# A decode step with grouped-query attention and a gated FFN: shorter tail arithmetic, an earlier drain of the last scores, and a repacked on-chip memory

## The chip, the core and the metric

The kernel runs on one core of one Trainium2 chip. The metric is the device time of one execution in microseconds (us), as the median of several. The profile is one execution seen by the hardware profiler; its span is about 1.7 us shorter than the device time of the same execution (708.6 and 710.3 for the kernel before).

## The reference

One token (x has shape 1x1x512) passes a layernorm, attention over a cache of 65,536 positions with 32 query and 8 key/value heads of 128, an output projection, a residual, a second layernorm and a gated FFN of width 1792:

```python
h  = x + A_ref(layernorm(x), k_cache, v_cache, wq, wo)      # softmax(q k / sqrt(128)) v, then wo
h2 = h + B_ref(layernorm(h), w_gate, w_up, w_down)          # (sigmoid(h wg) * (h wu)) wd
```

The caches are bf16, 134 MB each; all reads together are 282 MB. Streaming them is nearly all of the work.

## The kernel before

K and V come in 128 chunks of 2 MB (8 groups, 8 chunks of each kind per group), each as 128 rows of 16 KB, one per partition. One queue, the sync engine's, issues all of them in a fixed order. PE transposes each K chunk, DVE and ACT copy the result out of PSUM, and PE then multiplies by q ("T" and "S" below, S three blocks behind T). V chunks are multiplied by the softmax weights. The parts that the change touches:

```python
# tensors are placed one behind the other, in this order
x_row_b = SB([1, D], BF16);  x_row = SB([1, D], FP32);  xsq_row = SB([1, D], FP32)
...
h_row = SB([1, D], FP32);  h2_row = SB([1, D], FP32)
...
out_row_b = SB([1, D], BF16)
wo_sb = SB([P, H, D], BF16, "wo_sb")
# then 3 K buffers (the FFN weights lie over them), 6 staging tiles, 4 V buffers

# PE: the last three S blocks of a group are issued only when its V begins
def v_chunk(nv):
    if g not in v_started:
        drain_S((g + 1) * SBG)
        ...
# sync engine: FFN weights may land when the last S is done; V loads stand behind them
if fl and i >= idx_ffn:
    sp.wait_ge(sem_sprog, NSB)
    sp.dma_start(dst, srcap).then_inc(sem_wffn, 16)

# down projection: one row of 512, hT stationary
for f in range(NFC):
    mm = pe.matmul(ps_misc[0:1, 0:D], hT_b[:, f:f + 1], wd_sb[:, f, :], ...)
v.tensor_tensor(out=out_row_b, in0=ps_misc[0:1, 0:D], in1=h_row, op=ALU.add)
```

## Time and profile before

| | before |
|---|---|
| median of four runs, us | 710.65 (710.09 to 711.82) |
| span of the profiled run, us | 708.6 |
| mean DMA rate over the span, GB/s | 401 |
| busy share PE / DVE / ACT | 78% / 44% / 22% |
| last V chunk landed, us into the span | 688.7 |

A busy PE at 78% does not set the time here: the DMA engines are busy in nearly every slice. The views themselves are in the prediction below.

### The profile page before, as it was taken

How to read it: one execution, taken by the hardware profiler on the slowest of the kernel's cores; microseconds unless marked ns; L12 is line 12 of the kernel's file. 1: busy time of each engine (PE TensorE's matmuls, PEld its weight loads, DVE VectorE, ACT ScalarE, POOL GpSimd, SP SyncE). 2: the span in 40 equal slices, each digit the busy share in tenths (PEclk: the TensorE clock that was granted, in tenths of full speed). 3: DMA queues.
4: the chain of work that ended last, by engine and by line, in shares of the span. 5: the costliest groups of instructions: out<-in, count | busy, mean ns of one | idle time of the engine just before them, and what ended most of it. 6: DMA issues, size and time to landing. Idle time of an engine off the chain costs nothing.

```text
span 708.6 us, 26822 instructions
## 1 busy us (share of the span) xinstructions
PE 551.1 (78%) x12622; PEld 530.0 (75%) x12622; DVE 312.8 (44%) x498; ACT 158.9 (22%) x199; POOL 0.7 (0%) x7
## 2 busy tenths in 40 slices
PE   2987998869997798969887799869888689874235
PEld 2977998868996688968887788869788689863232
DVE  1755744427442654417442564417444464331002
ACT  0232522204221321204121222104122141212000
POOL 0000000000000000000000000000000000000000
PEclk9999877869777898869886697867877697765556
DMA  8999999999999999999999999999999999979970
GB/s 368 411 396 413 424 423 426 421 424 417 424 424 422 392 425 423 425 425 402 425 425 423 390 422 426 425 422 394 424 425 423 404 417 425 425 316 415 412 313 1
DMA packets 26162, 284.05 MB, mean 401 GB/s; under 512 B 2242, under 2 KB 8132, under 8 KB 9156
## 3 DMA queue, kind: packets, MB, share of 16 engines
q1 hardware_dynamic: 25780, 280.24, 94.6%
q8 instruction: 99, 1.62, 0.9%
q10 hardware_dynamic: 272, 2.10, 0.8%
q14 instruction: 11, 0.09, 0.0%
HBM read 282.33 MB, written 0.00 MB: 398 GB/s over the span
## 4 chain that ended last, share of the span: by engine, by line
PE 46%; DMA 44%; issue 6%; DVE 4%; ACT 0%; SPq 0%; DVEq 0%
DMA kin<-in_A_k_cache_dram 34%; PE ps_tr L576 28%; DMA v<-in_A_v_cache_dram 9%; PE ps_s L601 8%; PE ps_o L673 7%; DVE kts L408 1%; DVE pmax L442 1%; PE ps_misc L479 1%; DVE s L432 1%; PE ps_misc L721 1%; PE ps_misc L506 0%; ACT pt L532 0%; PE ps_misc L710 0%; PE ps_misc L715 0%; DVE diag L454 0%
## 5 line engine op out<-in xcount | busy, mean ns | idle before, releaser
L576 PE MATMUL ps_tr<-ident_b,kin 128*128 128x128 bf16 x4096 | 379.1, 246 | 60.1 <-issue 30.0
L408 DVE COPY kts<-ps_tr 128x1024 bf16<-128x1024 bf16 x384 | 258.3, 691 | 299.7 <-PE ps_tr L576 299.5
L576 PEld LDWEIGHTS ps_tr<-ident_b,kin 128*128 128x128 bf16 x4096 | 284.6, 110 | 68.5 <-issue 39.3
L419 ACT ACTIVATE kts<-ps_tr 128x1024 bf16<-128x1024 bf16 x128 | 130.8, 1022 | 469.5 <-PE ps_tr L576 469.5
L601 PE MATMUL ps_s<-qt_b,kts 128*128 128x4 bf16 x4096 | 184.5, 167 | 3.9 <-issue 3.7
L601 PEld LDWEIGHTS ps_s<-qt_b,kts 128*128 128x128 bf16 x4096 | 173.4, 102 | 1.8 <-issue 1.5
L673 PE MATMUL ps_o<-pt,v 128*128 128x4 bf16 x4096 | 119.6, 168 | 59.5 <-DMA v<-in_A_v_cache_dram 46.5
L673 PEld LDWEIGHTS ps_o<-pt,v 128*128 128x128 bf16 x4096 | 114.1, 98 | 65.4 <-DMA v<-in_A_v_cache_dram 48.0
L432 DVE COPY s<-ps_s 128x512 f32<-128x512 f32 x32 | 21.8, 681 | 10.7 <-PE ps_s L601 10.7
L532 ACT ACTIVATE pt<-s,nmax 128x512 bf16<-128x512 f32 x32 | 22.6, 710 | 14.7 <-DVE nmax L465 14.7
L515 DVE RECIPROCAL rs<-ps_misc 128x4 f32<-128x4 f32 x8 | 1.4, 174 | 46.9 <-PE ps_misc L684 46.9
L442 DVE TENSOR_REDUCE pmax<-s 128x4 f32<-128x2048 f32 x8 | 18.3, 2284 | 0.0
L735 ACT ACTIVATE stats<-stats,eps_c 1x1 f32<-1x1 f32 x1 | 0.3, 293 | 50.5 <-DVE stats L389 50.5
L499 PE MATMUL ps_misc<-ident_f,pmax 128*4 128x128 f32 x8 | 2.4, 297 | 11.5 <-DVE pmax L442 11.5
L479 PE MATMUL ps_misc<-wo_sb,aot_b 128*1 128x512 bf16 x32 | 9.9, 438 | 0.9 <-DVE aot_b L518 0.5
L499 PEld LDWEIGHTS ps_misc<-ident_f,pmax 128*4 128x4 f32 x8 | 0.6, 81 | 12.2 <-DVE pmax L442 12.2
L491 DVE TENSOR_TENSOR h_row<-ps_misc,h_row 1x512 f32<-1x512 f32 x7 | 4.8, 679 | 9.6 <-PE ps_misc L479 9.6
L555 PE MATMUL ps_misc<-xnT_b,wq_sb 128*128 128x1 bf16 x128 | 3.5, 165 | 6.5 <-DMA wq_sb<-in_A_wq_dram 6.5
L555 PEld LDWEIGHTS ps_misc<-xnT_b,wq_sb 128*128 128x128 bf16 x128 | 3.5, 104 | 6.6 <-issue 6.6
L532 ACT ACTIVATION_READ_ACCUMULATOR pt<-s,nmax 128x1 f32 x32 | 6.0, 189 | 0.0
L548 PE MATMUL ps_misc<-ident_b,xn_row_b 1*128 1x1 bf16 x4 | 0.3, 166 | 6.8 <-DVE xn_row_b L397 6.8
L548 PEld LDWEIGHTS ps_misc<-ident_b,xn_row_b 1*128 1x128 bf16 x4 | 0.2, 103 | 6.8 <-DVE xn_row_b L397 6.8
(51 smaller groups left out, 51.3 us busy)
## 6 DMA issues: line engine op xcount, KB each, us to landing
kin<-in_A_k_cache_dram SPq DMA_DIRECT2D x64, 2048.0 KB, 19.7
v<-in_A_v_cache_dram SPq DMA_DIRECT2D x64, 2048.0 KB, 24.2
wo_sb<-in_A_wo_dram SPq DMA_DIRECT2D x4, 1024.0 KB, 14.5
wq_sb<-in_A_wq_dram ACTq DMA_DIRECT2D x1, 2048.0 KB, 9.9
wq_sb<-in_A_wq_dram SPq DMA_DIRECT2D x1, 2048.0 KB, 12.2
wg_sb<-in_B_w_gate_dram SPq DMA_DIRECT2D x2, 896.0 KB, 7.7
wu_sb<-in_B_w_up_dram SPq DMA_DIRECT2D x2, 896.0 KB, 20.8
wd_sb<-in_B_w_down_dram SPq DMA_DIRECT2D x2, 896.0 KB, 21.9
```

The source lines that it names most:

```text
L408: v.tensor_copy(kt_stage[ss][:, :, :], ps_tr[bank][:, :].rearrange("p (t m) -> p t m", m=P)).then_inc(sem_evD, 1)
L419: act.activation(kt_stage[ss][:, :, :], ps_tr[bank][:, :].rearrange("p (t m) -> p t m", m=P), ACTF.Copy).then_inc(sem_evA, 1)
L432: v.tensor_copy(s_sb[sidx][:, :, b * BT:(b + 1) * BT], src).then_inc(sem_sevac, 1)
L442: v.tensor_reduce(out=pmax[sidx][:, :], in_=s_sb[sidx][:, :, :], axis=AX.X, op=ALU.max).then_inc(sem_pmax, 1)
L479: mm = pe.matmul(ps_misc[0:1, 0:D], aot_b[:, h:h + 1], wo_sb[:, h, :], start=(hh == 0), stop=(hh == R - 1))
L491: v.tensor_tensor(out=h_row[:, :], in0=ps_misc[0:1, 0:D], in1=h_row[:, :], op=ALU.add).then_inc(sem_hacc, 1)
L532: act.activation(pt_sb[sidx][:, j, :], s_sb[sidx][:, j, :], ACTF.Exp, bias=nmax[sidx][:, j:j + 1], scale=1.0, accum_out=rowsum[sidx][:, j: ...
L555: mm = pe.matmul(ps_misc[:, C_QT + h:C_QT + h + 1], wq_sb[:, c, h * P:(h + 1) * P], xnT_b[:, c:c + 1], start=(c == 0), stop=(c == NDC - 1))
L576: mm = pe.transpose(ps_tr[bank][:, i * P:(i + 1) * P], kin_buf[slot][:, t, :], ident_b[:, :])
L601: mm = pe.matmul(ps_s[bank][:, col:col + R], src_tiles[i], qt_b[:, g * R:(g + 1) * R], start=True, stop=True)
L673: mm = pe.matmul(ps_o[:, 0:R], v_buf[slot][:, t, :], pt_sb[sidx][:, :, tg], start=(tg == 0), stop=(tg == TG - 1))
L721: mm = pe.matmul(ps_misc[0:1, 0:D], hT_b[:, f:f + 1], wd_sb[:, f, :], start=(f == 0), stop=(f == NFC - 1))
```

## The change

The intent is to shorten what follows the last byte (layernorm by batch-norm statistics, down projection with the weights stationary, so that 56 one-column matmuls take the place of 14 of 512 columns) and to let the FFN weights start sooner (the last scores are drained right behind the last K chunk). Rows that are no longer needed are dropped, small tensors are added, and a pad is placed ahead of `wo_sb`.

```diff
-        x_row = SB([1, D], FP32, "x_row")
-        xsq_row = SB([1, D], FP32, "xsq_row")
...
-        h2_row = SB([1, D], FP32, "h2_row")
...
-        out_row_b = SB([1, D], BF16, "out_row_b")
+        hresT = SB([P, NDC], FP32, "hresT")
+        oT_f = SB([P, NDC], FP32, "oT_f")
+        out4_b = SB([NDC, P], BF16, "out4_b")
+        SB([P, 48], BF16, "pad0")
         wo_sb = SB([P, H, D], BF16, "wo_sb")
...  layernorm_row: two 512-element passes and three 1-element operations become
+            v.bn_stats(stats[:, 0:6], src)
+            v.bn_aggr(stats[:, 6:8], stats[:, 0:6])
...  k_chunk
+                if kc == NKC - 1:
+                    drain_S(NSB)
...  before the second layernorm's transposes: the residual is transposed too
+            for c in range(NDC):
+                mm = pe.matmul(ps_misc[:, C_HT + c:C_HT + c + 1], h_row[0:1, c * P:(c + 1) * P], ones_f[0:1, 0:1], ...)
...
-            for f in range(NFC):
-                mm = pe.matmul(ps_misc[0:1, 0:D], hT_b[:, f:f + 1], wd_sb[:, f, :], ...)
+            for blk in range(NDC):
+                for f in range(NFC):
+                    mm = pe.matmul(ps_misc[:, C_DN + blk:C_DN + blk + 1], wd_sb[:, f, blk * P:(blk + 1) * P], hT_b[:, f:f + 1], ...)
...  then add (128x4), transpose (4x128), copy, store as four rows
```

More of the change, by code (lines that the diff above doesn't have):

```diff
@@ L25 @@
     K_MODE="pe",
+    KDMA_FIRST=0,
+    V_EARLY=0,
+    V_EARLY_AT=2,
     V_QUEUE="sp",
@@ L83, in bass_sequential_preLN__gqa_block_cached__glu_gated_glu__decode_kernel @@
         modes = [kmode] * NKC
+    for kc in range(min(NKC, plan["KDMA_FIRST"])):
+        modes[kc] = "dma"
     assert all(m in ("pe", "dma") for m in modes)
@@ L108, in bass_sequential_preLN__gqa_block_cached__glu_gated_glu__decode_kernel @@
         x_row_b = SB([1, D], BF16, "x_row_b")
-        x_row = SB([1, D], FP32, "x_row")
-        xsq_row = SB([1, D], FP32, "xsq_row")
-        stats1 = SB([1, 8], FP32, "stats1")
-        stats2 = SB([1, 8], FP32, "stats2")
+        stats1 = SB([1, 16], FP32, "stats1")
+        stats2 = SB([1, 16], FP32, "stats2")
         xn_row_b = SB([1, D], BF16, "xn_row_b")
@@ L174, in bass_sequential_preLN__gqa_block_cached__glu_gated_glu__decode_kernel @@
         C_U = C_G + NFC
-        assert C_U + NFC <= 512
+        C_HT = C_U + NFC
+        C_DN = C_HT + NDC
+        C_OT = C_PMAXT
+        assert C_DN + NDC <= 512
         sem_kin = [SEM(f"sem_kin{i}") for i in range(NKIN)]
@@ L194, in bass_sequential_preLN__gqa_block_cached__glu_gated_glu__decode_kernel @@
         sem_hnT = SEM("sem_hnT")
+        sem_hTpe = SEM("sem_hTpe")
+        sem_hTc = SEM("sem_hTc")
+        sem_oTsb = SEM("sem_oTsb")
+        sem_oT = SEM("sem_oT")
         sem_ffn1 = SEM("sem_ffn1")
@@ L351, in _ @@
             idx_ffn = order.index(("V", G - 1, 0))
+            n_vearly = min(plan["V_EARLY"], NV, NCH) if (G > 1 and plan["V_QUEUE"] == "sp") else 0
             for i, (kind, g, c) in enumerate(order):
@@ L355, in _ @@
                     nk += 1
+                    if nk == plan["V_EARLY_AT"]:
+                        for j in range(n_vearly):
+                            issue_v(sp, j)
                 else:
-                    if plan["V_QUEUE"] == "sp":
+                    if plan["V_QUEUE"] == "sp" and nv >= n_vearly:
                         issue_v(sp, nv)
@@ L374, in _, with layernorm_row @@
             sp.wait_ge(sem_outsb, 1)
-            sp.dma_start(out[0, :, :], out_row_b[:, :]).then_inc(sem_out, 16)
+            sp.dma_start(out[0, 0, :].rearrange("(b p) -> b p", p=P), out4_b[:, :]).then_inc(sem_out, 16)
             sp.wait_ge(sem_out, 16)
-        def layernorm_row(v, src, dst_row32, dst_b, stats, sem_chain, sem_sqrt):
-            v.tensor_scalar(out=dst_row32[:, :], in0=src, scalar1=1.0, scalar2=0.0, op0=ALU.mult, op1=ALU.add,
-                            accum_out=stats[:, 0:1]).then_inc(sem_chain, 1)
+        def layernorm_row(v, src, dst_b, stats, sem_chain, sem_sqrt):
+            v.bn_stats(stats[:, 0:6], src).then_inc(sem_chain, 1)
@@ L381, in layernorm_row @@
             v.wait_ge(sem_chain, 1)
-            v.tensor_tensor_reduce(out=xsq_row[:, :], in0=dst_row32[:, :], in1=dst_row32[:, :], scale=1.0, scalar=0.0,
-                                   op0=ALU.mult, op1=ALU.add, accum_out=stats[:, 1:2]).then_inc(sem_chain, 1)
-            v.wait_ge(sem_chain, 2)
-            v.tensor_scalar(out=stats[:, 2:3], in0=stats[:, 0:1], scalar1=1.0 / D, scalar2=None, op0=ALU.mult).then_inc(sem_chain, 1)
+            v.bn_aggr(stats[:, 6:8], stats[:, 0:6]).then_inc(sem_chain, 1)
@@ L386, in layernorm_row @@
+            v.wait_ge(sem_sqrt, 1)
+            v.reciprocal(stats[:, 9:10], stats[:, 8:9]).then_inc(sem_chain, 1)
             v.wait_ge(sem_chain, 3)
-            v.tensor_tensor(out=stats[:, 3:4], in0=stats[:, 2:3], in1=stats[:, 2:3], op=ALU.mult).then_inc(sem_chain, 1)
+            v.tensor_scalar(out=stats[:, 10:11], in0=stats[:, 6:7], scalar1=-1.0, scalar2=stats[:, 9:10],
+                            op0=ALU.mult, op1=ALU.mult).then_inc(sem_chain, 1)
             v.wait_ge(sem_chain, 4)
-            v.tensor_scalar(out=stats[:, 4:5], in0=stats[:, 1:2], scalar1=1.0 / D, scalar2=stats[:, 3:4],
-                            op0=ALU.mult, op1=ALU.subtract).then_inc(sem_chain, 1)
@@ L391, in layernorm_row @@
-            v.wait_ge(sem_sqrt, 1)
-            v.reciprocal(stats[:, 6:7], stats[:, 5:6]).then_inc(sem_chain, 1)
-            v.wait_ge(sem_chain, 6)
-            v.tensor_scalar(out=stats[:, 7:8], in0=stats[:, 2:3], scalar1=-1.0, scalar2=stats[:, 6:7],
-                            op0=ALU.mult, op1=ALU.mult).then_inc(sem_chain, 1)
-            v.wait_ge(sem_chain, 7)
-            return v.tensor_scalar(out=dst_b[:, :], in0=dst_row32[:, :], scalar1=stats[:, 6:7], scalar2=stats[:, 7:8],
+            return v.tensor_scalar(out=dst_b[:, :], in0=src, scalar1=stats[:, 9:10], scalar2=stats[:, 10:11],
@@ L486, in f @@
                 if g == 0:
-                    v.wait_ge(sem_ln1, 8)
-                    v.tensor_tensor(out=h_row[:, :], in0=ps_misc[0:1, 0:D], in1=x_row[:, :], op=ALU.add).then_inc(sem_hacc, 1)
+                    v.wait_ge(sem_x, 16)
+                    v.tensor_tensor(out=h_row[:, :], in0=ps_misc[0:1, 0:D], in1=x_row_b[:, :], op=ALU.add).then_inc(sem_hacc, 1)
                 else:
@@ L543, in _ @@
         def _(pe):
-            pe.wait_ge(sem_ln1, 8)
+            pe.wait_ge(sem_ln1, 5)
             pe.wait_ge(sem_dsetup, 1)
@@ L700, in _ @@
             dve_prog.append(dve_hacc(G - 1))
-            pe.wait_ge(sem_ln2, 8)
+            pe.wait_ge(sem_hacc, G)
+            for c in range(NDC):
+                mm = pe.matmul(ps_misc[:, C_HT + c:C_HT + c + 1], h_row[0:1, c * P:(c + 1) * P], ones_f[0:1, 0:1],
+                               start=True, stop=True)
+            mm.then_inc(sem_hTpe, 1)
+            pe.wait_ge(sem_ln2, 5)
+            pe.wait_ge(sem_hTc, 1)
             for c in range(NDC):
@@ L718, in _ @@
             pe.wait_ge(sem_hT, 1)
-            pe.wait_ge(sem_hacc, G)
-            for f in range(NFC):
-                mm = pe.matmul(ps_misc[0:1, 0:D], hT_b[:, f:f + 1], wd_sb[:, f, :], start=(f == 0), stop=(f == NFC - 1))
+            for blk in range(NDC):
+                for f in range(NFC):
+                    mm = pe.matmul(ps_misc[:, C_DN + blk:C_DN + blk + 1], wd_sb[:, f, blk * P:(blk + 1) * P], hT_b[:, f:f + 1],
+                                   start=(f == 0), stop=(f == NFC - 1))
             mm.then_inc(sem_down, 1)
+            pe.wait_ge(sem_oTsb, 1)
+            pe.matmul(ps_misc[0:NDC, C_OT:C_OT + P], oT_f[:, :], ident_f[:, :], is_transpose=True,
+                      start=True, stop=True).then_inc(sem_oT, 1)
         @block.scalar
@@ L729, in _ @@
             act.wait_ge(sem_pool, 1)
-            act.wait_ge(sem_ln1, 5)
-            act.activation(stats1[:, 5:6], stats1[:, 4:5], ACTF.Sqrt, bias=eps_c[0:1, :], scale=1.0).then_inc(sem_sqrt1, 1)
+            act.wait_ge(sem_ln1, 2)
+            act.activation(stats1[:, 8:9], stats1[:, 7:8], ACTF.Sqrt, bias=eps_c[0:1, :], scale=1.0).then_inc(sem_sqrt1, 1)
             for f in act_prog:
                 f(act)
-            act.wait_ge(sem_ln2, 5)
-            act.activation(stats2[:, 5:6], stats2[:, 4:5], ACTF.Sqrt, bias=eps_c[0:1, :], scale=1.0).then_inc(sem_sqrt2, 1)
+            act.wait_ge(sem_ln2, 2)
+            act.activation(stats2[:, 8:9], stats2[:, 7:8], ACTF.Sqrt, bias=eps_c[0:1, :], scale=1.0).then_inc(sem_sqrt2, 1)
             act.wait_ge(sem_ffn1, 2)
@@ L743, in _ @@
             v.wait_ge(sem_x, 16)
-            layernorm_row(v, x_row_b[:, :], x_row, xn_row_b, stats1, sem_ln1, sem_sqrt1).then_inc(sem_ln1, 1)
+            layernorm_row(v, x_row_b[:, :], xn_row_b, stats1, sem_ln1, sem_sqrt1).then_inc(sem_ln1, 1)
             v.wait_ge(sem_xT, 1)
@@ L752, in _ @@
             v.wait_ge(sem_hacc, G)
-            layernorm_row(v, h_row[:, :], h2_row, hn_row_b, stats2, sem_ln2, sem_sqrt2).then_inc(sem_ln2, 1)
+            layernorm_row(v, h_row[:, :], hn_row_b, stats2, sem_ln2, sem_sqrt2).then_inc(sem_ln2, 1)
+            v.wait_ge(sem_hTpe, 1)
+            v.tensor_copy(hresT[:, :], ps_misc[:, C_HT:C_HT + NDC]).then_inc(sem_hTc, 1)
             v.wait_ge(sem_hnT, 1)
@@ L759, in _ @@
             v.wait_ge(sem_down, 1)
-            v.tensor_tensor(out=out_row_b[:, :], in0=ps_misc[0:1, 0:D], in1=h_row[:, :], op=ALU.add).then_inc(sem_outsb, 1)
+            v.wait_ge(sem_hTc, 1)
+            v.tensor_tensor(out=oT_f[:, :], in0=ps_misc[:, C_DN:C_DN + NDC], in1=hresT[:, :], op=ALU.add).then_inc(sem_oTsb, 1)
+            v.wait_ge(sem_oT, 1)
+            v.tensor_copy(out4_b[:, :], ps_misc[0:NDC, C_OT:C_OT + P]).then_inc(sem_outsb, 1)
     return nc
```

## The prediction

> **What bounds the kernel now.** I read the page's slices first, then the chain that ended last, then narrow windows around the one deep dip of the DMA, then the sync engine's waits, and last the timeline there and at the end.
>
> The slices (each 17.7 us) show a kernel that streams its caches:
>
> ```profile
> DMA  8999999999999999999999999999999999979970
> GB/s 368 411 396 413 424 423 426 421 424 417 424 424 422 392 425 423 425 425 402 425 425 423 390 422 426 425 422 394 424 425 423 404 417 425 425 316 415 412 313 1
> ```
>
> The DMA is full nearly everywhere, at about 424 GB/s. So only three places can give time: the start, the dip to 316 in slice 36 (620 to 638 us), and the stretch after the last byte. The change leaves bytes and the order of transfers alone, so the 600 us of streaming should stay as they are.
>
> Windows around the dip (the last columns are granted clock, DMA share, GB/s):
>
> ```profile
> 628.00:630.00 2.00, 1.49 (x56) 1.49 (x56) 0.00 (x0) 0.00 (x0) 0.00 (x0) 0.90 1.06 451
> 630.00:632.00 2.00, 0.41 (x16) 0.32 (x13) 0.00 (x0) 0.00 (x0) 0.00 (x0) 0.50 0.64 270
> 632.00:634.00 2.00, 1.82 (x62) 1.76 (x63) 0.00 (x0) 0.00 (x0) 0.00 (x0) 0.50 0.51 205
> 634.00:636.00 2.00, 1.00 (x22) 1.00 (x22) 0.00 (x0) 0.00 (x0) 0.00 (x0) 0.50 0.37 156
> 636.00:638.00 2.00, 0.32 (x13) 0.24 (x9) 1.61 (x4) 0.00 (x0) 0.00 (x0) 0.50 0.38 53
> 638.00:640.00 2.00, 0.37 (x1) 0.08 (x1) 1.54 (x1) 0.00 (x0) 0.00 (x0) 0.50 0.90 358
> ```
>
> The share falls to one half at 630, not to zero. Half of the 16 engines have run out of work while the others are still busy; only about 636.5 to 638 is idle for all. The cause is in the sync engine's waits and in the timeline (start us, length us):
>
> ```profile
> SPq L366 <- PE ps_s L601: 16.7, 1, 16.7
> ...
> 635.54 0.78 PE L601 MATMUL ps_s<-qt_b,kts 128*128 128x4 bf16 x24
> 636.35 0.38 SPq L366 DMA_DIRECT2D wg_sb<-in_B_w_gate_dram  x1
> 636.78 0.77 SPq L338 DMA_DIRECT2D v<-in_A_v_cache_dram  x1
> ```
>
> The FFN weights overlay the K buffers, so their first load waits for the last score matmuls. Those three leftover blocks (24 matmuls) stand behind three V chunks in PE's order and end at 636.3, although the last K transposes ended at 625.6. V loads behind that DMA in the same queue wait with it.
>
> The end, in the chain:
>
> ```profile
> 688.71 0.05 issue
> 688.76 1.87 PE ps_o L673 x64
> ...
> 694.14 0.69 DVE h_row L379 x2
> 694.83 0.02 issue
> 694.85 0.68 DVE xsq_row L382
> ...
> 698.03 1.65 PE ps_misc L710 x56
> ...
> 701.66 4.68 PE ps_misc L721 x14
> 706.34 0.02 issue
> 706.36 0.68 DVE out_row_b L760
> ```
>
> From the last V landing (688.71) to the end of the span (708.6) lie 19.9 us in which nothing runs beside the chain. What is saved there is saved in full.
>
> **What the Trainium skill says.** "DMA: Bandwidth & Descriptors", section "Queues, rings and completion order": a copy is split over rings of up to 16 engines, each of which takes its descriptors in ring order, and nothing aligns the engines. The trace agrees: its landing records, one per engine, spread from 631.0 to 637.0 us for the last chunk before the dip (eight engines by 632.3, eight from 635.2 on), but only from 640.5 to 641.1 for the first transfer after it. "TensorE: Matmul & The Clock Gate", section "Back-to-back issue gap": about N/1.2 ns per matmul at the low clock for N moving columns, and a floor of about 25 ns for small N. The trace agrees: the 512-column matmuls of L721 stand 0.43 us apart while the clock is 0.5, and 56 one-column matmuls of L710 take 1.65 us, 29.5 ns each. "VectorE: DVE Perf Modes", section "Rules for kernel authors": in chained operations, lower their count rather than their semaphores. The trace agrees: operations on a single element take 0.14 to 0.20 us each. No page gives a time for the batch-norm statistics instructions.
>
> **The change part by part.**
>
> (a) Layernorm by batch-norm statistics. In the second layernorm, 694.11 (h_row done) to 697.46 (hn_row_b done) is 3.35 us. It loses two 512-element passes (0.69 and 0.68) and three one-element operations (0.15, 0.16, 0.21), with a gap of about 0.02 each. It gains one statistics pass and one aggregation. The pass reads 512 f32 elements on one partition as L382 does, so I take 0.66; the aggregation is tiny, I take 0.20 from the slowest one-element row. New sum, with gaps: 0.68 + 0.22 + root 0.33 + reciprocal 0.19 + scale 0.24 + apply 0.54 = 2.20. Saved: 1.15 us. The first layernorm gains as much but is hidden: its result waits until 13.5 us for the wq weights. Worth 0.
>
> (b) The residual is transposed for the new output layout. Four small PE transposes of h_row run beside the layernorm. But DVE copies them out (128x4 from PSUM, 0.17 as L755) after hn_row_b, and PE waits for that copy before the hn transposes. On the path: +0.19 us.
>
> (c) Down projection with the weights stationary: 14 matmuls of 512 columns become 56 of one column, the same form as L710, so 1.65 instead of 4.68 us. The final add becomes 128x4 (0.18 as L758, instead of 0.68), and there follow a PE transpose of 4x128 f32 (0.37 to 0.39, as L499 at this clock) and a DVE copy of 4x128 out of PSUM (0.26, near L450's 0.28). Old: 4.68 + 0.02 + 0.68 = 5.38. New with gaps: 1.65 + 0.02 + 0.18 + 0.05 + 0.39 + 0.02 + 0.26 = 2.57. Saved: 2.8 us. The output DMA now has four rows of 256 B instead of one of 1 KB; I count it as equal.
>
> (d) The leftover scores are drained right after the last K chunk. The last ACT eviction ends at 626.7, so the scores end near 627, and the first FFN load is issued there instead of at 636.35. The following V loads need V chunks consumed at about 629, 631 and 635 us, all before the queue empties, so the dip disappears. What is that worth? Summing one minus the DMA share over 629.5 to 638.5 gives 4.4 us of mean engine time. But the last V chunk lands with its slowest engine, and those eight had run out only at 637.0. The seven V chunks (4.9 us each in the landings), four gate and up pieces (2.2) and two down pieces (2.6) that remain are 48.3 us of an undisturbed engine's work: 637.0 + 48.3 = 685.3, against 688.71. Saved: 3.4. The landings also show single engines of the slow half set back by about 1.2 us in turn, three times after 638 (about 654, 669, 684). Five of the eight had had their turn by 637, so I expect the next three to meet engines with slack. For a one-in-three chance that one of them does not, I take off 0.4: 3.0 us. PE pays 1.3 us more wait before the three V chunks, but they wait on DMA until 632.1 anyway.
>
> (e) The dropped rows move the buffers in SBUF; the added pad keeps their offset within 64 bytes, so I expect no effect. The new plan switches are all zero and emit nothing.
>
> Sum: 1.15 - 0.19 + 2.8 + 3.0 = 6.8 us. 710.65 - 6.8 = 703.9 us.
>
> **The rivals.** First: the engines even out and the whole 4.4 us returns. For it: the dip in the share is that large. Against it: each engine has a fixed part of each chunk, and the share stays at one half for 5 us without the working half getting faster. It makes 702.5. Second: the dip only moves, because a later V load then waits for its buffer. The fifth load of the last group needs its first V chunk consumed, which waits for the softmax of that group; that begins only after group 6's normalisation on DVE, about 1.2 us earlier than before. For it: this wait was real (issued at 646.3). Against it: by then some 10 MB are queued, enough until 654 even on the fast engines. It makes 707. Third: the column-wise down projection is slower than L710, because 14 steps accumulate into one PSUM column. For it: nothing ran in exactly this form. Against it: L673 accumulates 64 steps into the same four columns at 29 ns each. At double cost it makes 705.5.
>
> **Range and chances.** The tail terms are read off like rows and should be right to 0.6 us together. The DMA term can be 0 to 4.4, mostly 2.2 to 4.4. Runs scatter by 0.9 us around the median. So 702.0 to 706.3 should hold it eight times in ten. Faster by over 2% would need 14.2 us, more than both idle places offer: 0.02. Within 2%: 0.97. Slower by over 2%: 0.01, for an effect of the moved buffers on the streaming.
>
> **What would show it.** Right: slice 36 back near 420 GB/s, no half-share windows around 632, the FFN load issued near 627, last V landing near 685.5, then about 16.1 us to the end, with the down projection near 1.65 us and the layernorm near 2.2. The landings would stay about 6 us apart in the last group. Wrong: a new dip between 640 and 660, a statistics pass well over 0.7 us, 56 matmuls well over 1.7 us, a longer output DMA, or a changed rate in the streaming.

## More of the kernel before

One line more is needed later, the window from 250 to 310 us, which has no turn between groups in it (the last column is GB/s):

```profile
250.00:310.00 60.00, 50.45 (x1211) 48.85 (x1208) 25.34 (x38) 12.28 (x12) 0.00 (x0) 0.82 1.01 425
```

## The result

The changed kernel takes 696.14 us (median of eight runs, 696.07 to 698.59) against 711.07 for the kernel before (twelve runs). The ratio is 0.9794, with a 95% interval from 0.978 to 0.9808. A ratio here is the record's, worked out from the fast runs of the same rounds; it is within 0.0004 of the ratio of their means and not quite the ratio of the medians. The gain of 14.9 us is more than twice the predicted 6.8, and the time lies outside the predicted range of 702.0 to 706.3.

First the slices of the page of the changed kernel (17.4 us each):

```profile
DMA  8999999999999999999999999999999999999980
GB/s 365 420 418 420 422 431 425 427 429 420 427 427 428 404 428 428 429 427 407 429 424 429 412 417 426 429 427 406 428 425 430 429 389 427 428 425 426 419 352 3
```

The deep dip is gone, as predicted. But the streaming also runs a little higher everywhere: most slices show 425 to 430 where the kernel before showed 422 to 425, and slices 3 and 4, in which the output weights begin to load, show 418 and 420 instead of 396 and 413. The same window as above, 250 to 310 us, in the changed kernel:

```profile
250.00:310.00 60.00, 49.84 (x1165) 48.29 (x1162) 22.24 (x33) 11.20 (x11) 0.00 (x0) 0.76 1.01 428
```

Windows around the place of the dip, which had stood at about half the DMA share (next to last column) from 630 us on:

```profile
626.00:628.00 2.00, 0.01 (x1) 0.01 (x1) 0.00 (x0) 0.00 (x0) 0.00 (x0) 0.50 1.05 439
628.00:630.00 2.00, 1.25 (x28) 1.16 (x27) 0.68 (x3) 0.00 (x0) 0.00 (x0) 0.50 0.98 413
630.00:632.00 2.00, 0.07 (x1) 0.08 (x1) 1.87 (x1) 0.00 (x0) 0.00 (x0) 0.50 0.99 420
```

The sync engine's waits and the timeline of the changed kernel there. The wait for the scores has shrunk from 16.7 to 7.6 us, and the next V load now waits for its own buffer, not for the FFN weights:

```profile
SPq L382 <- PE ps_s L608: 7.6, 1, 7.6
...
619.55 0.35 PE L608 MATMUL ps_s<-qt_b,kts 128*128 128x4 bf16 x8 [0.54 <-ACT kts L426]
619.93 0.38 SPq L382 DMA_DIRECT2D wg_sb<-in_B_w_gate_dram  x1
622.92 0.33 SPq L350 DMA_DIRECT2D v<-in_A_v_cache_dram  x1
```

And the chain that ended last, after the last V landing:

```profile
678.25 0.05 issue
678.29 1.87 PE ps_o L682 x64
...
683.67 0.69 DVE stats L395
684.36 0.02 issue
684.39 0.18 DVE stats L397
...
685.34 0.53 DVE hn_row_b L404
685.87 0.08 DVE hresT L774
685.96 0.14 issue
686.09 0.25 PE ps_misc L718 x4
...
690.22 1.66 PE ps_misc L736 x56
...
692.54 0.28 DVE out_b L784
```

Where the 14.2 us of span came from can be read from three landmarks:

| landmark, us into the span | before | after | gain in the stretch |
|---|---|---|---|
| first V chunk of the last group has landed on its slowest DMA engine | 637.0 | 629.5 | 7.4 |
| last V chunk landed | 688.7 | 678.25 | 3.0 (51.7 becomes 48.7) |
| end of the span | 708.6 | 694.4 | 3.7 (19.9 becomes 16.15) |

The second and third stretch are what the prediction had (3.0 and 3.76). The first, 7.4 us in the streaming, was put at zero. The trace's own packet records say what changed there:

| DMA packets in the trace | before | after |
|---|---|---|
| 16 KB cache rows (16,384), median, and share at exactly 611 ns | 614 ns, 9% | 611 ns, 98% |
| the same, mean of those under 700 ns | 615.6 ns | 611.1 ns |
| 1 KB rows of the output and down weights, mean | 50.1 ns | 46.2 ns |
| 16 KB instruction packets (99), mean | 1070 ns | 932 ns |

Each engine moves 1,024 of the cache rows, so 4.5 ns each are 4.6 us. The 1 KB rows give 5,890 x 3.9 ns / 16 = 1.4 us. If the instruction packets fall on eight of the engines, as the turns in the landings suggest, each of those saves another 99/8 x 138 ns = 1.7 us. The sum, 7.7 us, is an estimate from these records. About 6.9 of it fall before the first landmark (121 of the 128 chunks, 4,096 of the 1 KB rows, nearly 90 of the instruction packets), near the 7.4 seen.

What could change packets all over? The addresses in the compiled programs do differ: the output weights, K, FFN, q and V buffers all start 32 bytes past a multiple of 512 in the kernel before (K at 88,096) and exactly on one in the changed kernel (K at 81,408). So theory A is the place of the buffers. Theory B is that the new arithmetic or the new order sped up the streaming.

### The profile page after: what moved, and what is told of

Read it like the earlier page. It is cut to its first block, busy times and chain, and to the rows that moved or that the text cites. A ratio compares the mean times of both kernels' runs of the same rounds, so it can differ in the third digit from the quotient of the medians.

```text
span 694.4 us, 26917 instructions
## 1 busy us (share of the span) xinstructions
PE 551.2 (79%) x12673; PEld 533.0 (77%) x12673; DVE 310.6 (45%) x490; ACT 159.0 (23%) x199; POOL 0.7 (0%) x7
## 4 chain that ended last, share of the span: by engine, by line
PE 45%; DMA 43%; issue 6%; DVE 4%; ACT 1%; SPq 0%; DVEq 0%
DMA kin<-in_A_k_cache_dram 34%; PE ps_tr L583 28%; DMA v<-in_A_v_cache_dram 9%; PE ps_s L608 8%; PE ps_o L682 7%; DVE kts L415 1%; DVE pmax L449 1%; PE ps_misc L486 1%; ACT pt L539 1%; DVE s L439 1%; PE ps_misc L513 0%; PE ps_misc L736 0%; PE ps_misc L725 0%; PE ps_misc L730 0%; DVE diag L461 0%
## 5 line engine op out<-in xcount | busy, mean ns | idle before, releaser
L539 ACT ACTIVATE pt<-s,nmax 128x512 bf16<-128x512 f32 x32 | 22.6, 710 | 14.3 <-DVE nmax L472 14.2
L486 PEld LDWEIGHTS ps_misc<-wo_sb,aot_b 128*1 128x1 bf16 x32 | 2.2, 87 | 4.0 <-issue 1.7
```

What stands on the lines that cost most here:

```text
L486: mm = pe.matmul(ps_misc[0:1, 0:D], aot_b[:, h:h + 1], wo_sb[:, h, :], start=(hh == 0), stop=(hh == R - 1))
L539: act.activation(pt_sb[sidx][:, j, :], s_sb[sidx][:, j, :], ACTF.Exp, bias=nmax[sidx][:, j:j + 1], scale=1.0, accum_out=rowsum[sidx][:, j: ...
```

## The experiments

Twelve kernels ran, each three rounds beside the kernel before on the same chip, all correct.

| run | edit | median, us | ratio | 95% |
|---|---|---|---|---|
| e1_pad512 | before + 480 B pad | 702.06 | 0.9873 | 0.9848 to 0.9898 |
| e2_off32 | after, pad 32 B longer | 704.94 | 0.9910 | 0.9890 to 0.9930 |
| e3_drain | before + drain | 709.00 | 0.9966 | 0.9948 to 0.9984 |
| e4_tail | after - drain, pad 32 B longer | 707.46 | 0.9946 | 0.9926 to 0.9966 |
| e5_off64 | before + 32 B pad | 711.37 | 1.0003 | 0.9982 to 1.0025 |
| e6_off256 | before + 224 B pad | 703.36 | 0.9891 | 0.9868 to 0.9914 |
| e7_v_only | before + 480 B ahead of V | 707.59 | 0.9965 | 0.9940 to 0.9989 |
| e8_nv5 | after, five V buffers | 696.56 | 0.9796 | 0.9781 to 0.9811 |
| e9_off128 | before + 96 B pad | 709.86 | 0.9980 | 0.9955 to 1.0006 |
| e10_nodrain | after - drain | 697.18 | 0.9801 | 0.9775 to 0.9826 |
| e11_wd8 | after, one wd load in 16 parts (sync) | 700.43 | 0.9836 | 0.9813 to 0.9859 |
| e12_wd8_act | the same, issued by ACT | 700.30 | 0.9838 | 0.9821 to 0.9854 |

### The place of the buffers, done alone and undone alone

```diff
e1_pad512, in the kernel before:
+        SB([P, 240], BF16, "pad0")
         wo_sb = SB([P, H, D], BF16, "wo_sb")
e2_off32, in the changed kernel:
-        SB([P, 48], BF16, "pad0")
+        SB([P, 64], BF16, "pad0")
```

> The kernel before with 480 unused bytes put in front of the weight and cache buffers, so that they start at a multiple of 512 B as in the changed kernel (before they start 32 B past one). Nothing else changes. Theory A (the place of the buffers sped up every transfer, about 7.4 us up to the landing of the first V chunk of the last group, and about 0.5 us after it): 7 to 8.5 us faster than the kernel before, ratio 0.988 to 0.990, and 16 KB packets near 611 ns without a tail of longer ones. Theory B (the streaming gained for another reason in the change, such as fewer vector instructions or the order on PE): no change, ratio 1.000.

> The changed kernel with its pad 32 B longer, so that the buffers start 32 B past a multiple of 512 B as in the kernel before. Theory A: loses the 7 to 8.5 us again, about 704, which is what the prediction (703.9) would have been without its error on the placement; ratio to before 0.990. Theory B: stays at 696, ratio 0.979.

The pad alone made the kernel before 9 us faster (0.0127 x 711), slightly beyond the expected band, without one instruction changed. Its window from 250 to 310 us shows the rate of the changed kernel:

```profile
250.00:310.00 60.00, 47.94 (x1175) 46.20 (x1172) 22.60 (x34) 11.25 (x11) 0.00 (x0) 0.81 1.01 428
```

Its 16 KB packets stand at 611 ns in 97% of the cases. Moving the changed kernel's buffers by 32 B cost 8 us (0.9910 against 0.9794) and brought the packets back to a median of 614 ns. Theory B falls. The second run lands at 704.94: this is the change as the prediction understood it, and the prediction had 703.9.

### Which boundary it is

```diff
e5_off64, e9_off128, e6_off256: in the kernel before, ahead of wo_sb
+        SB([P, 16], BF16, "pad0")     # 64 B past a multiple of 512
+        SB([P, 48], BF16, "pad0")     # 128 B past
+        SB([P, 112], BF16, "pad0")    # 256 B past
```

> The kernel before with the buffers 64 B past a multiple of 512 B instead of 32. Theory A1 (what counts is a boundary of 64 B): the whole gain of the 512 B pad, about 9 us, ratio 0.987, 16 KB packets at 611 ns. Theory A2 (what counts is a larger boundary, 128 B or more): no gain or a part, ratio 0.993 to 1.000. Both leave everything else as it is.

> The kernel before with the buffers 256 B past a multiple of 512 B. If boundaries up to 256 B count but not 512 B: the whole gain, about 9 us, ratio 0.987. If only 512 B counts: none. If a boundary of 64 B is all: the whole gain here as well as at 64.

> The kernel before with the buffers 128 B past a multiple of 512 B. Runs at 32 and 64 B gained nothing and at 256 and 0 B about 8 to 9 us. If a packet is cut at boundaries of 256 B (16 KB in 65 pieces instead of 64): no gain here, ratio 1.000, 16 KB packets again at 613 to 621 ns. If the boundary that counts is 128 B: about 8.5 us, ratio 0.988.

Starts at 64 and 128 B past a multiple of 512 gain nothing that these runs can tell (1.0003 and 0.9980, both intervals contain 1); 256 B past gains like 512 (0.9891 against 0.9873, intervals overlap). The boundary is 256 B. The packets alone show a small slope below it: the mean of the 16 KB rows under 700 ns is 615.6, 614.6 and 614.1 ns at 32, 64 and 128 B past, and 611.1 at 256. The window at 64 B past, then at 256 B past:

```profile
250.00:310.00 60.00, 49.69 (x1190) 47.74 (x1186) 25.86 (x39) 12.29 (x12) 0.00 (x0) 0.84 1.01 425
```

```profile
250.00:310.00 60.00, 47.36 (x1164) 45.62 (x1161) 22.06 (x34) 11.24 (x11) 0.00 (x0) 0.80 1.01 427
```

The Trainium skill has a mechanism that fits, in "DMA: Bandwidth & Descriptors", section "How a descriptor splits into AXI transactions": a transaction moves up to 256 B and must start from a 256 B boundary, so a row whose length is a multiple of 256 B takes one transaction more when it does not start on a boundary. The page tells this of reading; that the written side, which is the unaligned one here, is split likewise is not shown by these runs. Counted so, a 16 KB row takes 65 instead of 64, 1.6% more; a 1 KB row of the output and down weights 5 instead of 4, 25%; a 3.5 KB row of the gate and up weights 15 instead of 14, 7% (estimates from the page). In the traces of the kernel before and the changed one, nine tenths of the packets stay within 621 ns against 611 (1.6%), 56 against 46 (22%) and 149 against 140 (6%). So the slow packets of three sizes agree with the page. The mean of the 16 KB rows is only 0.7% up; why most unaligned packets pay part of the cost is not shown.

### V alone

```diff
e7_v_only, in the kernel before, behind the K buffers and staging tiles:
+        SB([P, 240], BF16, "padV")
         wq_sb = transient("wq_sb", [P, NDC, HD], BF16)
```

> The kernel before with a pad of 480 B in front of the V buffers alone: V (and wq) at a multiple of 512 B; K, the output weights and the FFN weights still 32 B past one. V is 64 of the 128 cache transfers. If the cost is one of each transfer by its own place: about half the gain, 3.5 to 4.5 us, ratio 0.994, and two kinds of 16 KB packets in about equal number. If one class of transfer alone matters, none or all of it.

The gain is 2.5 us by the ratio and 3.3 by the medians, somewhat less than half. The packets did not split evenly: 77% stand at 611 ns, although only half of the transfers were moved. Even if every V row is among them, so are more than half of the K rows, against 9% in the kernel before. Unaligned K packets too became faster where V packets were aligned: the cost is not strictly each transfer's own. How it is shared is not shown. The 1 KB rows (49.9 ns) and instruction packets (1056 ns) stayed slow, which fits the smaller gain.

### The drain and the tail, each by itself

```diff
e3_drain, in the kernel before (k_chunk); e10_nodrain and e4_tail take it away again:
+                if kc == NKC - 1:
+                    drain_S(NSB)
```

> The kernel before with only the early drain of the last scores. Theory A (landing is set by the slowest DMA engine, which lost 1.9 us idle plus turns of delay): 3.0 us faster, ratio 0.9958, the last landings 5 to 6 us apart by engine. Rival (the whole 4.4 us of mean engine time comes back): ratio 0.9938. If the drain was also behind the streaming gain: 10 us, ratio 0.986.

> The changed kernel without the early drain and with the buffers 32 B past a multiple of 512 B: only the layernorm and the down projection are changed. Theory A: 3.7 us faster than before, ratio 0.9948, all of it after the last V landing. Rival (something in the head or the streaming depends on these parts): more than 5 us.

> The changed kernel without the early drain, buffers on the 512 B boundary. The drain alone gave 2.3 us in the kernel before and 2.5 between two runs with the other parts, where the prediction had 3.0. If it is worth the same with the faster transfers: 698.3 to 699.2, ratio 0.983. If the faster transfers make the dip cost more: 700 or above.

The tail is worth 3.8 us (0.0054 x 711), as expected. The drain is worth 2.4 us in the kernel before (1.1 to 3.7 by the interval), 2.6 between e4_tail and e2_off32 (0.9946 and 0.9910), but only 0.5 to 1.0 between e10_nodrain and the changed kernel, inside both intervals. The expectation for e10_nodrain (698.3 to 699.2) was missed. The 2.6 cannot be put down to the drain, either: in the two profiled executions e4_tail's slowest engine was already 2.6 us behind at the 51st of the 64 V chunks (593.9 against 591.3 us), long before the drained scores. The windows of e10_nodrain show the same dip as the kernel before had, in the mean of the engines:

```profile
624.00:626.00 2.00, 1.57 (x58) 1.58 (x59) 0.00 (x0) 0.00 (x0) 0.00 (x0) 0.50 0.45 188
626.00:628.00 2.00, 1.50 (x38) 1.42 (x34) 0.46 (x1) 0.00 (x0) 0.00 (x0) 0.50 0.43 180
...
627.54 0.38 SPq L382 DMA_DIRECT2D wg_sb<-in_B_w_gate_dram  x1
```

So a dip of the same depth cost almost nothing. The landing records tell why: its slowest engine finished at 629.4, 1.9 us after the FFN load was issued, and the FFN piece, which takes 2.15 us of an engine, landed there at 632.0: 0.5 us idle. In the kernel before, the load was issued only 0.6 us ahead of the slowest engine's end and that engine idled for 1.9 us. There, PE had also stood still for 1.1 us within the last V chunk of group 6, in a gap that the profile puts down to no wait; in e10_nodrain that gap is absent. Two more traces without the drain fit. The stretch is the time from the landing of the first V chunk of the last group on its slowest engine to the last landing:

| no drain | gap in PE, us | idle of the slowest engine, us | stretch, us |
|---|---|---|---|
| before | 1.1 | 1.9 | 51.7 |
| e1_pad512 | 1.1 | 2.6 | 52.2 |
| e4_tail | none | 0.4 | 50.4 |
| e10_nodrain | none | 0.5 | 49.4 |

With the drain the stretch is 48.7 us in the changed kernel, 48.9 in e3_drain and 49.9 in e2_off32. So the mean share of the DMA does not tell what a dip costs; the slowest engine's idle time comes much nearer. That the gap makes the FFN load late is read from these traces alone: no run set the gap on purpose, and why two executions have it is not shown.

### Attempts at a faster kernel

```diff
e8_nv5, in the changed kernel:
-    NV=4,
+    NV=5,
e11_wd8 and e12_wd8_act, in the changed kernel, for the first of the two wd loads:
+            for p0 in range(0, P, 32):
+                for j in range(4):
+                    ps = slice(p0 + j, p0 + 32, 4)
+                    sp.dma_start(dst[ps], srcap[ps]).then_inc(sem_wffn, 16)     # act.dma_start in e12
```

> The changed kernel with five V buffers instead of four; the bytes freed by the change make room for it. An attempt at a faster kernel: the remaining dips of the DMA at the seven turns between groups (shares of 0.75 to 0.95 in one or two windows of 4 us each) come from the queue waiting for buffers. If deeper buffering fills them: 1 to 3 us faster than 696.1, ratio to before 0.975 to 0.978. If the slowest DMA engine never ran dry there: no change, 0.979.

The bytes that the change freed hold a fifth V buffer, but it gave nothing (696.56 against 696.14). It did not fill the dips at the turns between groups either: in windows of 4 us the lowest shares are 0.75, 0.86 and 0.88 in the changed kernel and 0.79, 0.81 and 0.89 here. So V buffers are not what these dips wait for, and what filling them would be worth is not shown.

> The changed kernel with one of the two down-projection loads (0.9 MB, 2.6 us of every engine) cut into 16 transfers of 8 rows, which then run on eight DMA engines instead of 16. The end waits for the slowest engine, and eight engines run about 5 us behind the other eight. If the eight that get the load are the early ones: the last landing comes about 2.6 us earlier, 693.5, ratio 0.976, and the spread of the last landings shrinks to 0 to 1 us. If they are the late ones: 2.6 us later, 698.7, ratio 0.983, spread 10 us. If the spread does not set the end: 696.1.

> As the run before it with 16 transfers of 8 rows for one down-projection load, but issued by the scalar engine, idle at that time. In that run the sync engine spent 20.6 us on issuing the 16 (638.1 to 658.7), the next V load waited behind them, and the early engines ran dry, so it told nothing about the spread. Now the V loads are not held up. If the eight engines that get the load are the early ones: about 693.5, ratio 0.976, spread of the last landings 0 to 1 us. If they are the late ones: about 698.7, ratio 0.983, spread about 10 us.

Both came out about 4 us slower than the changed kernel. In the first the sync engine was busy for 20.6 us with issuing the 16 parts, with the next V load behind them (eleven of the parts took 0.68 to 0.84 us each, the other five 1.0 to 3.7, why is not shown):

```profile
638.12 20.57 SPq L325 DMA_DIRECT2D wd_sb<-in_B_w_down_dram  x16
658.73 0.44 SPq L360 DMA_DIRECT2D v<-in_A_v_cache_dram  x1
```

In the second, with the V loads free, the last landings spread over 9.1 us: two engines at 673 us, twelve from 677.0 to 679.8, two at 682, where the changed kernel has eight by 673.0 and eight from 676.4 on. Each part did run on eight engines, by the count of the landing records (nine per part, as the output store of four rows leaves five and that of one row two). But the eight were neither all early nor all late: six early and two late ones would give the landings seen. That is an inference; the trace does not name the engines. The spread of about 6 us at the end remains. If both halves ended together, about half of it could be won (an estimate from 6.2), and no version here beats the changed kernel.

## Why the prediction was wrong

**The step that failed is (e)**: "The dropped rows move the buffers in SBUF; the added pad keeps their offset within 64 bytes, so I expect no effect." Both halves are wrong. I had summed the sizes in the source, by which the buffers move 6,720 bytes, a multiple of 64; the compiled program rounds each tensor up to 32 B, they move 6,688, and so went from 32 B past a multiple of 512 to the multiple itself. And the place matters: e1_pad512 and e2_off32 measured 9 and 8 us for it, more than all the other parts together. With it fell the step before, that 600 us of streaming would stay as they are: 7.4 us were gained there. This term was left at zero, and it is the miss: with the buffers moved back (e2_off32) the changed kernel took 704.94, where 703.9 had been predicted. (That the new switches are all zero is a slip; one is 2, without effect.) The profile of before could not show it, because every transfer had the same handicap and 424 GB/s looked like the limit. The address list of the built kernel and the page's section on transactions could have.

**(a) to (c), the tail**, were right: the statistics pass took 0.69 (0.66 expected) and the aggregation 0.18 (0.20); the layernorm became 2.22 instead of 2.20. Waiting for the residual's copy cost 0.17 instead of 0.19. The 56 matmuls took 1.66 instead of 1.65, and everything from there to the output copy's end 2.60 instead of 2.57. From the last landing to the end it took 16.15 us where 16.1 had been said.

**(d), the drain**, was right in mechanism: the first FFN load left right after the last scores, no new dip appeared, and the last landings stayed 6.2 us apart, as said. In the profiled pair the stretch shortened by exactly the predicted 3.0 us, which is partly luck: some of it belongs to the faster transfers. By itself the drain measured 2.4 us in the kernel before and 0.5 to 1.0 with the faster transfers. The prediction took the slowest engine's idle time from one execution; it was 0.4 to 2.6 us in four traces without the drain, so the term was not as fixed as it looked. The first rival (4.4 us, the mean of all engines) is excluded by e3_drain, whose interval ends at 0.9948, 3.7 us. The second rival (the dip moves) and the third (slow accumulation) did not happen.

**The chances** followed the range: 0.02 was given to faster by over 2%, and the ratio, 0.9794, lies just on that side, with an interval that reaches over the line. An effect of the moved buffers had been thought of only as a loss, at 0.01. The reason given for the 0.02 does not hold as worded: the idle places it had read, 4.4 us of dip and 19.9 of tail, are more than 14.2 together; only what the change takes from them is less.

## What to carry to other kernels

When a change adds or drops on-chip tensors, compare the buffer addresses of the two built programs before believing that only the arithmetic changed; in a kernel bound by transfers, try the buffers that a DMA writes on a multiple of 256 B, which took 224 B of padding here (e6_off256) and gave 8 of 711 us. A dip in the mean share of the DMA engines cost about what the slowest engine lost in it, far less than the dip's area in e10_nodrain. The dependent chain of small operations after the last transfer could be predicted row by row to a tenth of a microsecond.

## What the Trainium skill lacked or had wrong

- "DMA: Bandwidth & Descriptors", section "How a descriptor splits into AXI transactions", gives the 256 B rule with the example of fetched bytes. It doesn't say whether it holds for the start of an SBUF destination or what it costs in a stream: here 16 KB rows went from 611.1 to 615.6 ns in the mean and 1 KB rows from 46.2 to 50.1, worth 8 to 9 us of 711 for 284 MB. None of the page's rules for kernel authors asks for aligned buffers.
- "SBUF — State Buffer", section "Operand start alignment", says of its runs that they timed nothing. The runs here time four unaligned or partly aligned starts: 32, 64 and 128 B past a multiple of 512 cost 8 to 9 us (the 128 B start perhaps 1 us less), 256 B costs nothing that could be told.
- "DMA: Bandwidth & Descriptors", section "Queues, rings and completion order", has no number for how far engines drift apart: here 5.1 to 7.5 us in nine traces after about 630 us, in two halves of eight, with single engines of the late half set back by about 1.2 us in turn.
- No page has the time of the batch-norm statistics instructions: 0.69 us for 512 f32 elements on one partition and 0.18 us for the aggregation.
- No page has the cost of cutting a load of 0.9 MB into 16 loads of 8 strided rows: 20.6 us on the sync engine (0.68 us for most of them, up to 3.7 for some), where the issue of the whole load takes 0.43.
